# Attention with cluster masks: running sums in SBUF, separate product banks, logits in a score tile, and numbering at the head of a pair

## The chip, the cores and the metric

The kernel runs on one core of a Trainium2 chip. The metric is the device time of one execution in microseconds (us); lower is better. The engines are named as in the profile: PE (TensorE), ACT (ScalarE), DVE (VectorE), POOL (GpSimd) and SP (SyncE, which here issues nearly all DMAs).

## The reference

Routing attention over 4 batches, 8 heads, 768 positions and 64 dimensions is followed by a two-layer network with a squared ReLU. All is float32.

```python
q_assign = argmax(q_n @ c_n.T); k_assign = argmax(k_n @ c_n.T)    # 16 clusters per head
mask = q_assign[:, :, :, None] == k_assign[:, :, None, :]
scores = where(mask, scale * q @ k.T, -1e9)
attn = softmax(scores); x = attn @ v          # then (B*S, H*D) = 3072 x 512
out = square(maximum(x @ w_in, 0)) @ w_out    # w_in 512 x 2048, w_out 2048 x 512
```

## The kernel before

The order of the instructions is written out by hand: each engine runs its instructions in the order of the code and blocks at the first one whose inputs aren't there. That holds for SP too, so a DMA that waits holds all DMAs behind it.

**Attention** goes over 16 pairs of heads (p = 0 to 15; one pair is two heads of one batch, side by side in 128 partitions). The scores stand transposed: keys in the partitions, queries in the columns. A pair has nine score tiles of two banks (ps_sc, three buffers): tiles 0 to 5 hold one block of 128 keys by 512 queries for both heads, tiles 6 to 8 hold two blocks of keys by the last 256 queries. For each tile (tile_of, L558) PE multiplies mask rows (L450) and q, k (L441), and ACT takes the exponential (L457) into one of nine ex tiles. After the nine tiles PE multiplies the exponentials with v (times_v, L474): 24 products of 512 columns into bank V, then 24 of 256 columns into bank M. ACT copies each result into xT (evict, L483). V and M are the two halves of one tile of two banks, vm.

**Sums.** DVE adds the exponentials up over the keys (add, L460): five adds of 128x1024 for tiles 0 to 5 run in vm and the fifth writes total; three more adds take tiles 6 to 8 through part into total. At the end of the pair PE sums total over its partitions (add_up, L492) into M; at the start of the next pair DVE transposes and inverts these (invert, L501, L505), and SP sends them out and back, spread over the partitions (far_r, L507; rb, L510). finish (L520) multiplies them into xT in the next pair.

**Masks.** The cluster of each position comes from logits (L334, PE), a transpose of these (turn_logits, L344, DVE) and number (L346 to L392, DVE), which writes the clusters as small marks. SP writes the marks out (far, L382) and reads them back as six rows (rows, L387), which the masks of the next pair multiply. Pair 0 has its masks turned by PE instead (turn_onehot).

**Turned q and k.** Pairs 0 and 1 are turned by PE (turn_first, turn). From pair 2 on ACT splits q and k into 16-bit words (split_words, L314), SP writes these (L315) and reads them back with a transposing DMA (turn_words, L326).

**Weights.** In each pair one block of 128x512 of w_in is rounded in three steps: round_1 on ACT (L138, L139), round_2 on DVE (L145, L148, L152) and round_3 on POOL (L160). load_ahead (L130, SP) loads the blocks into three buffers, so block p + 2 needs the buffer of block p - 1, which round_3(p - 1) frees.

**The network** comes after attention, as seven products of halves in place of eight (L739 up, L791 down) for four blocks; the first block is multiplied while the rest of the weights is rounded.

In the loop over p, SP's order in one pair from pair 2 on is: second words (L315), q and k (L99), the transposing read for pair p + 2 (L326), v (L109), far_r (L507), two rb (L510), first words (L315), far (L382), six rows (L387), weights (L130), and again the second words. The quotation below has the line numbers of the profile.

Of the kernel before, what the change touches and what calls it, by code (L numbers as in the profile page):

```python
# [18 lines left out]
P = 128  # L19
# [6 lines left out]
def kernel(  # L26
# [44 lines left out]
    expp = att.enter_context(tc.tile_pool(name="expp", bufs=9))  # L71
    accp = att.enter_context(tc.tile_pool(name="accp", bufs=1))
    ps_sc = att.enter_context(tc.tile_pool(name="ps_sc", bufs=3, space=PSUM))
    ps_vm = att.enter_context(tc.tile_pool(name="ps_vm", bufs=1, space=PSUM))
    vm = ps_vm.tile([P, 2, 512], F32, name="vm")
    V, M = vm[:, 0], vm[:, 1]


    BY_PE = 2
# [63 lines left out]
    def round_2(i):  # L143
        dst, lo, hi = of_block(i)
        nc.vector.scalar_tensor_tensor(  # L145
            out=lo, in0=hi, scalar=0x80000000, in1=lo, op0=ALU.bitwise_and, op1=ALU.bitwise_or
        )
        nc.vector.tensor_scalar(  # L148
            out=hi.bitcast(F32), in0=dst.bitcast(F32), scalar1=2.0 ** -15, scalar2=HIGHEST,
            op0=ALU.max, op1=ALU.min,  # L150
        )
        nc.vector.tensor_scalar(  # L152
            out=dst, in0=hi, scalar1=3, scalar2=None, op0=ALU.logical_shift_left
        )

    def round_3(i):
        dst, lo, hi = of_block(i)
        raw_w.pop(i)
        dst, lo = dst.bitcast(I32), lo.bitcast(I32)
        nc.gpsimd.tensor_tensor(out=dst, in0=dst, in1=lo, op=ALU.add)  # L160
# [61 lines left out]
    def fixed_rows():  # L222
        for i, (row, value) in enumerate(((2.0, 1.0), (0.0, -BIG))):
            nc.vector.tensor_scalar(
                out=fixed[:, i : i + 1], in0=row_i[:, 1:2], scalar1=row, scalar2=value,
                op0=ALU.is_equal, op1=ALU.mult,
            )
        for t in rows_of:
            nc.gpsimd.memset(t, 0.0)
            for i in range(2):  # L230
                nc.vector.tensor_scalar(
                    out=t[:, i], in0=t[:, i], scalar1=fixed[:, i : i + 1], scalar2=None,
                    op0=ALU.add,
                )
# [31 lines left out]
    def centroids_turned():  # L266
        nc.tensor.transpose(
            out=M[:, 0:P], in_=cn.rearrange("p e d -> p (e d)"), identity=ident
        )
        nc.vector.tensor_copy(out=cnT, in_=M[:, 0:P])  # L270
# [4 lines left out]
    def turn_first(which):  # L275
        if which == 0:
            qkT[0] = qktp.tile([P, 2 * NCH, P], F32, name="qkT")
        pt = ps_sc.tile([P, 2, 512], F32, name="sc")
        for c in range(NCH):
            nc.tensor.transpose(  # L280
                out=pt[:, c // NB, (c % NB) * P : (c % NB + 1) * P], in_=raw[0][which][:, c],
                identity=ident,
            )
        for i, copy in enumerate((nc.scalar.copy, nc.vector.tensor_copy)):
            c = NCH * which + NB * i
            copy(out=qkT[0][:, c : c + NB].rearrange("p c n -> p (c n)"), in_=pt[:, i, 0:TB])
        if which == 1:
            raw.pop(0)

    def turn(pair, part, bank):  # L290
        if part == 0:
            qkT[pair] = qktp.tile([P, 2 * NCH, P], F32, name="qkT")
        for i in range(4):
            which, c = divmod(4 * part + i, NCH)
            nc.tensor.transpose(
                out=bank[:, P * i : P * (i + 1)], in_=raw[pair][which][:, c], identity=ident
            )
        (nc.scalar.copy if part == 2 else nc.vector.tensor_copy)(
            out=qkT[pair][:, 4 * part : 4 * part + 4].rearrange("p c n -> p (c n)"), in_=bank
        )  # L300
        if part == 2:
            raw.pop(pair)
# [28 lines left out]
    def logits(pair, bank):  # L331
        hp = pair % HP
        for g in range(4):
            nc.tensor.matmul(  # L334
                bank[32 * g : 32 * g + 32, 0:TB], lhsT=cnT[:, 2 * C * hp : 2 * C * (hp + 1)],
                rhs=qkT[pair][:, NB * g : NB * (g + 1)], start=True, stop=True,
            )


    lt = {}  # L340

    def turn_logits(pair, bank):
        lt[pair] = once.tile([P, 2 * NBL, C], F32, name="lt")
        nc.vector.transpose(out=lt[pair].rearrange("p n c -> p (n c)"), in_=bank[:, 0:TB])  # L344

# [48 lines left out]
    def turn_onehot():  # L394
        spare = expp.tile([P, 2, 512], F32, name="ex").bitcast(BF16)
        ohT[0] = spare.rearrange("p a n -> p (a n)")[:, 0 : 2 * S].rearrange(
            "p (a n) -> p a n", a=2
        )
        half = NBL // 2
        for part, bank in ((0, V), (1, M)):  # L400
            po = bank.bitcast(BF16)[:, 0 : half * P].rearrange("p (b g i) -> p b g i", b=half, g=4)
            for b in range(half):
                nc.tensor.transpose(
                    out=po[:, b].rearrange("p g i -> p (g i)"),
                    in_=oh[:, half * part + b].rearrange("p e c -> p (e c)"), identity=ident_b,
                )
            for which in range(2):
                dst = ohT[0][:, which].rearrange("p (g b i) -> p b g i", g=2, b=NBL)
                dst = dst[:, half * part : half * (part + 1)]
                src = po[:, :, 2 * which : 2 * which + 2]  # L410
                if which == 0:
                    nc.vector.tensor_copy(out=dst, in_=src)
                else:
                    nc.scalar.activation(out=dst, in_=src, func=ACT.Copy, bias=-BIG, scale=BIG)
# [16 lines left out]

    def begin(i):
        sc[i] = ps_sc.tile([P, 2, 512], F32, name="sc")


    def score(pair, i, j, first):
# [135 lines left out]

    centroids_norm()
    turn_first(0)
    centroids_turned()
    turn_first(1)
    logits(0, V)
    turn_logits(0, V)
    number(0)
    fixed_rows()  # L580

    first_sums = []
    x_early, w_early = x_sums(FEED[0]), []
    for p in range(NG):
        load_qk(p + 3)
        load_ahead(0)
        if p:
            turn_words(p + 2)
        load_v(p + 1)
        if p == HP + 1:  # L590
            nc.sync.dma_start(x_far, xT.pop(0))
        if p:
            invert(p - 1)
        if 2 < p + 1 < NG:
            turn_logits(p + 1, V)
        if p:
            round_2(p - 1)
            round_3(p - 1)


        if p == 0:
            for i in range(NB):
                begin(i)
                score(p, i, 0, True)
            turn_onehot()
            for i in range(NB):
                mask(p, i, 0, False)
                exponential(i)
            for i, bank in enumerate((V, M, V)):
                turn(1, i, bank)  # L610
        else:
            for i in range(NB):
                tile_of(p, i)
        if p < 2:
            logits(p + 1, M)
            turn_logits(p + 1, M)
        total[p] = endp.tile([P, 2, S], F32, name="total")
        first, last = total[p][:, :, 0:QA], total[p][:, :, QA:S]
        add(nc.vector, vm, ex[0], ex[1])
        add(nc.vector, vm, vm, ex[2])  # L620
        for i in range(NB, NCH):
            tile_of(p, i)
            add(nc.vector, vm if i < NCH - 1 else first, vm, ex[i])
        if p == 0:
            split_words(2, 0)
            split_words(2, 1)
            turn_words(2)
        split_words(p + 3, 0)
        if p + 1 < NG:
            number(p + 1)  # L630


        for i in range(NCH, NCH + NB):
            tile_of(p, i)
        load_ahead(p)
        part = accp.tile([P, 2, 512], F32, name="part")
        add(nc.vector, part, ex[NCH], ex[NCH + 1])
        add(nc.vector, part, part, ex[NCH + 2])
        add(nc.vector, last, part[:, :, 0:QB], part[:, :, QB : 2 * QB])
        if p:  # L640
            finish(p - 1)
        round_1(p)


        for i in range(NCH):
            times_v(p, i, V)
        evict(p, 0, V)
        split_words(p + 3, 1)
        for i in range(NCH, NCH + NB):
            times_v(p, i, M)  # L650
        raw_v.pop(p)
        if 2 < p + 2 < NG:
            logits(p + 2, V)
        evict(p, NCH, M)
        if p + 1 < NG:
            add_up(p, M)
        for d in (qkT, ohT):
            d.pop(p)
        if p >= NG - 2:
            for _ in range(2):  # L660
                if (found := next(x_early)) is not None:
                    first_sums.append(found)
            w_early.append(w_sums(len(w_early)))
# [390 lines left out]
```

## Time and profile before

| what | us |
|---|---|
| median of 3 runs (988.16 to 990.62) | 989.4 |
| the profiled execution | 983.46 |
| its span, first to last instruction | 981.7 |
| attention, from the start to the end of pair 15's v products | 386.5 |
| first up products, with the rounding of weights, to | 475.6 |
| the rest of the products, to the end | 981.7 |

Some rows of the costliest groups (line, engine, operation, output<-input, shape, count, then busy us and mean ns):

| group | busy us | mean ns |
|---|---|---|
| L457 ACT ex<-sc 128x1024, 144 times | 144.4 | 1025 |
| L441 PE sc<-qkT, 768 times, in pairs that run side by side | 160.7 | 501 |
| L474 PE vm<-ex,v_raw, 768 times, likewise | 130.9 | 490 |
| L460 DVE vm<-vm,ex 128x1024, 48 times | 59.2 | 1233 |
| L460 DVE vm<-ex 128x1024, 16 times | 24.1 | 1505 |
| L460 DVE part<-part,ex 128x1024, 16 times | 19.6 | 1225 |
| L460 DVE part<-ex 128x1024, 16 times | 19.0 | 1188 |

How to read it: a time in such a table is that of the engine alone; whether it counts depends on what waits for it. A row of waits names the engine and line that waited, after the arrow who released it, then us in total, how often, and the longest. In a list by time the first column is the start in us from the beginning of the span and the second the length; SPq is the queue in which SP issues DMAs, and its length is that of the issue, not of the transfer. In a list by stretches the columns are the length, busy us and number of instructions of PE, PE's weight loads, DVE, ACT and POOL, the granted clock, the share of the DMA engines and GB/s. From part 6 of the page: one words transfer is 384 KB, one block of weights 512 KB, q, k and v 384 KB each, rb 192 KB each, a row 1.5 or 3 KB.

### The profile page before, as it was taken

How to read it: one execution, taken by the hardware profiler on the slowest of the kernel's cores; microseconds unless marked ns; L12 is line 12 of the kernel's file. 1: busy time of each engine (PE TensorE's matmuls, PEld its weight loads, DVE VectorE, ACT ScalarE, POOL GpSimd, SP SyncE). 2: the span in 40 equal slices, each digit the busy share in tenths (PEclk: the TensorE clock that was granted, in tenths of full speed). 3: DMA queues.
4: the chain of work that ended last, by engine and by line, in shares of the span. 5: the costliest groups of instructions: out<-in, count | busy, mean ns of one | idle time of the engine just before them, and what ended most of it. 6: DMA issues, size and time to landing. Idle time of an engine off the chain costs nothing.

```text
span 981.7 us, 11662 instructions
## 1 busy us (share of the span) xinstructions
PE 920.3 (94%) x4471; PEld 594.8 (61%) x4471; DVE 580.1 (59%) x905; ACT 313.3 (32%) x455; POOL 148.3 (15%) x171
## 2 busy tenths in 40 slices
PE   6789997998998899899899999999999999999997
PEld 4344443554344444456788655888556888556886
DVE  5657775776777776699933565532566531656331
ACT  3555664665756445288000111000111000111000
POOL 2000100000000022475001331002231002231000
PEclk8899998999999999999999999999999999999999
DMA  8356666565566421243100000000000000000000
GB/s 226 82 134 171 197 180 194 153 180 168 153 172 164 105 70 47 81 140 101 60 22 22 22 1 1 11 22 21 11 1 0 22 22 22 1 0 1 22 23 24
DMA packets 102495, 74.80 MB, mean 76 GB/s; under 512 B 60064, under 2 KB 93088, under 8 KB 102176
## 3 DMA queue, kind: packets, MB, share of 16 engines
q1 hardware_dynamic: 100720, 73.55, 26.6%
q8 instruction: 37, 0.61, 0.3%
q10 hardware_dynamic: 1712, 0.43, 0.2%
q14 instruction: 26, 0.21, 0.1%
HBM read 43.73 MB, written 19.22 MB: 64 GB/s over the span
## 4 chain that ended last, share of the span: by engine, by line
PE 65%; DVE 17%; DMA 6%; ACT 5%; SPq 3%; issue 3%; POOL 0%; DVEq 0%; ACTq 0%; POOLq 0%
PE bank L791 29%; PE bank L739 23%; DVE vm L460 7%; PE vm L474 7%; ACT ex L457 3%; PE sc L441 3%; DMA far<-marks_t 3%; SPq L387 3%; DVE g L698 2%; DVE total L460 2%; DMA rows<-far 2%; DVE w_raw L148 1%; DVE w_raw L145 1%; PE sc L450 1%; DMA far_r<-seen 1%
## 5 line engine op out<-in xcount | busy, mean ns | idle before, releaser
L457 ACT ACTIVATE ex<-sc 128x1024 f32<-128x1024 f32 x144 | 144.4, 1025 | 65.1 <-PE sc L441 60.6
L698 DVE TENSOR_TENSOR g<-bank,g 128x384 f32<-128x384 f32 x192 | 103.4, 555 | 98.8 <-PE bank L739 91.2
L441 PE MATMUL sc<-qkT 64*128 64x512 f32 (+1 forms) x768 | 160.7, 501 | 0.0
L474 PE MATMUL vm<-ex,v_raw 128*64 128x512 f32 (+1 forms) x768 | 130.9, 490 | 19.9 <-ACT xT L483 11.6
L791 PE MATMUL bank<-w_out,g 128*128 128x256 f32 x576 | 127.3, 379 | 3.7 <-DVE g L532 3.7
L791 PEld LDWEIGHTS bank<-w_out,g 128*128 128x128 f32 x576 | 109.2, 190 | 19.8 <-DVE g L532 4.1
L474 PEld LDWEIGHTS vm<-ex,v_raw 128*64 128x64 f32 x768 | 52.3, 137 | 97.6 <-issue 45.7
L698 DVE TENSOR_TENSOR osb<-bank,osb 128x256 f32<-128x256 f32 x72 | 29.4, 423 | 134.6 <-PE bank L791 124.0
L441 PEld LDWEIGHTS sc<-qkT 64*128 64x128 f32 x768 | 79.0, 192 | 34.9 <-issue 27.8
L739 PE MATMUL bank<-xT,w_in 128*128 128x384 f32 x256 | 94.0, 490 | 3.2 <-DVE g L698 3.2
L739 PE MATMUL bank<-xT,w_s 128*128 128x384 f32 x256 | 94.1, 491 | 0.0
L739 PE MATMUL bank<-x_t,w_s 128*128 128x384 f32 x256 | 93.0, 486 | 0.0
L791 PE MATMUL bank<-w_t,g_s 128*128 128x256 f32 x384 | 86.8, 379 | 0.0
L791 PE MATMUL bank<-w_t,g 128*128 128x256 f32 x384 | 86.8, 379 | 0.0
L450 PE MATMUL sc<-rows 64*128 64x512 bf16 (+1 forms) x360 | 73.4, 329 | 13.2 <-DMA rows<-far 13.2
L552 POOL TENSOR_TENSOR w_s<-w_in 128x256 f32<-128x256 f32 x32 | 25.2, 789 | 363.2 <-PE bank L791 226.4
L791 PEld LDWEIGHTS bank<-w_t,g 128*128 128x128 f32 x384 | 73.0, 190 | 9.9
L791 PEld LDWEIGHTS bank<-w_t,g_s 128*128 128x128 f32 x384 | 73.0, 190 | 9.9
L702 ACT COPY osb<-bank 128x256 f32<-128x256 f32 x12 | 4.5, 372 | 219.0 <-PE bank L791 219.0
L160 POOL TENSOR_TENSOR w_in<-w_in,w_raw 128x512 int32<-128x512 int32 x16 | 20.9, 1308 | 349.8 <-DVE w_in L152 349.8
L739 PEld LDWEIGHTS bank<-xT,w_in 128*128 128x128 f32 x256 | 48.4, 190 | 37.4 <-DVE g L698 4.1
L702 ACT COPY g<-bank 128x384 f32<-128x384 f32 x32 | 15.2, 475 | 173.8 <-PE bank L739 173.8
(122 smaller groups left out, 997.3 us busy)
## 6 DMA issues: line engine op xcount, KB each, us to landing
words<-flat SPq DMA_DIRECT2D x28, 384.0 KB
w_raw<-in_moe_w_in_dram SPq DMA_DIRECT2D x16, 512.0 KB
w_raw<-in_moe_w_out_dram SPq DMA_DIRECT2D x16, 512.0 KB
v_raw<-in_v_dram SPq DMA_DIRECT2D x16, 384.0 KB
rb<-far_r SPq DMA_DIRECT2D x32, 192.0 KB
out_dram<-osb SPq DMA_DIRECT2D x23, 256.0 KB
q_raw<-in_q_dram SPq DMA_DIRECT2D x14, 384.0 KB
k_raw<-in_k_dram SPq DMA_DIRECT2D x14, 384.0 KB
```

The source lines that it names most:

```text
L160: nc.gpsimd.tensor_tensor(out=dst, in0=dst, in1=lo, op=ALU.add)
L387: nc.sync.dma_start(rows[D * e + row : D * e + row + 1, which].rearrange("p w (g b i) -> p (w g) b i", g=2, b=NBL), mine[2 * which.start : ...
L441: nc.tensor.matmul(sc[i][:, e, cols], lhsT=qkT[pair][rows, NCH + c], rhs=qkT[pair][rows, n.start // P : n.stop // P], start=first, stop=no ...
L450: nc.tensor.matmul(sc[i][:, e, cols], lhsT=ohT[pair][rows, 1, c * P : (c + 1) * P], rhs=ohT[pair][rows, 0, columns(i)], start=first, stop= ...
L457: nc.scalar.activation(out=ex[i], in_=sc.pop(i), func=ACT.Exp, scale=SCALE)
L460: eng.tensor_tensor(out=out, in0=a, in1=b, op=ALU.add)
L474: nc.tensor.matmul(bank[D * e : D * (e + 1), 0 : n.stop - n.start], lhsT=raw_v[pair][:, e, c], rhs=ex[i][:, e, cols], start=c == 0, stop=c ...
L552: nc.gpsimd.tensor_tensor(out=s1, in0=a[1][0], in1=a[1][1], op=ALU.add)
L698: nc.vector.tensor_tensor(out=out, in0=bank, in1=to, op=ALU.add)
L702: nc.scalar.copy(out=c11, in_=bank)
L739: nc.tensor.matmul(bank, lhsT=operands[j][0][:, kk], rhs=operands[j][1][:, kk], start=(kk == 0), stop=(kk == H2 - 1),)
L791: nc.tensor.matmul(bank, lhsT=left[:, f], rhs=right[:, f], start=(f == 0), stop=(f == F2 - 1))
```

## The change

- V and M become two tiles of one bank each (av_a, av_b) instead of halves of one tile.
- The running sum of tiles 0 to 5 stands in total, in SBUF, from the first add on.
- A tenth score tile is taken in each pair but the last: its bank 0 holds the logits of pair p + 2, its bank 1 the sums of pair p. add_up stands ahead of evict of M.
- number(p + 1) stands at the head of pair p, behind turn_logits, instead of behind the fifth add; for pairs 1 and 2 it stands behind the first add of the pair before. Its seven DMAs move with it in SP's order, ahead of both words.
- round_2 and round_3 of block p - 1 move from the head of pair p to behind finish. The load of block p + 2 now stands ahead of them in the code; on SP it waits for this pair's round_3.
- At the start both halves of pair 0 are turned first, all copies of turned pairs but one go to ACT, pair 1 is turned between the first scores of pair 0, fixed_rows stands behind the exponentials, and of the words of pairs 2 and 3 only the first stand ahead of the last three tiles.

```diff
-    ps_vm = att.enter_context(tc.tile_pool(name="ps_vm", bufs=1, space=PSUM))
-    vm = ps_vm.tile([P, 2, 512], F32, name="vm")
-    V, M = vm[:, 0], vm[:, 1]
+    ps_av = att.enter_context(tc.tile_pool(name="ps_av", bufs=1, space=PSUM))
+    V, M = (ps_av.tile([P, 512], F32, name=f"av_{i}") for i in "ab")
...
-        for i, copy in enumerate((nc.scalar.copy, nc.vector.tensor_copy)):
+        for i in range(2):
+            copy = nc.vector.tensor_copy if which and i else nc.scalar.copy
...
-        (nc.scalar.copy if part == 2 else nc.vector.tensor_copy)(
+        nc.scalar.copy(
...
-    def turn_logits(pair, bank):
+    def turn_logits(pair):
+        bank = sc["ls"][:, 0]
...
     centroids_norm()
     turn_first(0)
+    turn_first(1)
     centroids_turned()
-    turn_first(1)
-    logits(0, V)
-    turn_logits(0, V)
+    logits(0, begin("ls"))
+    turn_logits(0)
     number(0)
-    fixed_rows()
...
         if 2 < p + 1 < NG:
-            turn_logits(p + 1, V)
-        if p:
-            round_2(p - 1)
-            round_3(p - 1)
+            turn_logits(p + 1)
+            number(p + 1)
...
             for i in range(NB):
+                if i < 2:
+                    turn(1, i, (V, M)[i])
+                else:
+                    turn_onehot()
                 begin(i)
                 score(p, i, 0, True)
-            turn_onehot()
+                if i == 1:
+                    turn(1, 2, V)
             for i in range(NB):
                 mask(p, i, 0, False)
                 exponential(i)
-            for i, bank in enumerate((V, M, V)):
-                turn(1, i, bank)
+            fixed_rows()
...
-        if p < 2:
-            logits(p + 1, M)
-            turn_logits(p + 1, M)
...
-        add(nc.vector, vm, ex[0], ex[1])
-        add(nc.vector, vm, vm, ex[2])
+        add(nc.vector, first, ex[0], ex[1])
+        if p < 2:
+            logits(p + 1, begin("ls"))
+            turn_logits(p + 1)
+            number(p + 1)
+        add(nc.vector, first, first, ex[2])
         for i in range(NB, NCH):
             tile_of(p, i)
-            add(nc.vector, vm if i < NCH - 1 else first, vm, ex[i])
-        if p == 0:
-            split_words(2, 0)
-            split_words(2, 1)
-            turn_words(2)
-        split_words(p + 3, 0)
-        if p + 1 < NG:
-            number(p + 1)
+            add(nc.vector, first, first, ex[i])
+        split_words(2 if p == 0 else p + 3, 0)
...
         if p:
             finish(p - 1)
+            round_2(p - 1)
+            round_3(p - 1)
+        if p == 0:
+            split_words(2, 1)
+            turn_words(2)
+            split_words(3, 0)
         round_1(p)
...
-        if 2 < p + 2 < NG:
-            logits(p + 2, V)
+        if p + 1 < NG:
+            bank = begin("ls")
+            if 2 < p + 2:
+                if p + 2 < NG:
+                    logits(p + 2, bank)
+            add_up(p, bank[:, 1])
         evict(p, NCH, M)
-        if p + 1 < NG:
-            add_up(p, M)
```

More of the change, by code (lines that the diff above doesn't have):

```diff
@@ L334, in logits @@
             nc.tensor.matmul(
-                bank[32 * g : 32 * g + 32, 0:TB], lhsT=cnT[:, 2 * C * hp : 2 * C * (hp + 1)],
+                bank[32 * g : 32 * g + 32, 0, 0:TB], lhsT=cnT[:, 2 * C * hp : 2 * C * (hp + 1)],
                 rhs=qkT[pair][:, NB * g : NB * (g + 1)], start=True, stop=True,
@@ L433, in begin @@
         sc[i] = ps_sc.tile([P, 2, 512], F32, name="sc")
+        return sc[i]
     def score(pair, i, j, first):
```

## The prediction

> **What bounds the kernel now.** I read the page first, then TensorE's waits, then SyncE's own queue in order of time, then the stretches by clock.
>
> From the page, part 1, the busy times by engine, and from part 2 the granted clock:
>
> ```profile
> PE 920.3 (94%) x4471; PEld 594.8 (61%) x4471; DVE 580.1 (59%) x905; ACT 313.3 (32%) x455; POOL 148.3 (15%) x171
> ...
> PEclk8899998999999999999999999999999999999999
> ```
>
> TensorE is close to full over the span, but the average hides two parts. From 475.6 to the end (506.1 us) it is busy for 500.5 us in dense products that the change doesn't touch. All that can be won lies in attention, 0 to 386.5 us. There the waits of TensorE (total us, times, longest) are:
>
> ```profile
> PE sc L450 <- DMA rows<-far: 13.2, 11, 2.5
> PE vm L474 <- ACT xT L483: 11.6, 16, 1.3
> PE vm L474 <- DVE total L460: 8.4, 15, 1.0
> PE vm L492 <- ACT xT L483: 7.3, 15, 0.5
> ```
>
> The last three, 27.3 us, come from the shared tile vm: a pair waits 0.96 us for the last sum (first v product), 0.69 for the copy of V and 0.49 for that of M. From 96.21 to 117.98 one pair takes 21.77, so TensorE's own work in it is 21.77 - 2.14 = 19.63. That looks like a gain of 2.1 us a pair. The first row speaks against it: in 11 pairs TensorE waited for the mask rows, which come through SyncE. SyncE's queue over one pair (start, us, line):
>
> ```profile
> 95.30 0.46 SPq L315 DMA_DIRECT2D words<-flat  x1
> ...
> 100.30 3.21 SPq L326 DMA_TRANSPOSE qkT<-words  x1
> 103.61 0.53 SPq L109 DMA_DIRECT2D v_raw<-in_v_dram  x1
> 104.23 0.41 SPq L507 DMA_DIRECT2D far_r<-seen  x1
> 107.10 1.14 SPq L510 DMA_DIRECT2D rb<-far_r  x2
> 108.30 0.58 SPq L315 DMA_DIRECT2D words<-flat  x1
> 110.02 0.34 SPq L382 DMA_DIRECT2D far<-marks_t  x1
> 112.28 3.98 SPq L387 DMA_DIRECT2D rows<-far  x6
> 116.37 0.35 SPq L130 DMA_DIRECT2D w_raw<-in_moe_w_in_dram  x1
> 116.77 0.43 SPq L315 DMA_DIRECT2D words<-flat  x1
> ```
>
> This is a closed loop, because SyncE issues in order and blocks: words to transposition 5.0 (the words must land; 4.8 to 5.4 in all pairs from pair 2 on), its issue 3.3, v 0.6, far_r to rb 2.9, two rb 1.2, words 0.6, far to rows, six rows 4.1, weights 0.4. Far to rows is 1.5 to 2.3 where far follows words late and 3.4 where it follows at once (202.89 to 206.32). With 3.4 the loop is 21.5, beside 21.77 for TensorE with its waits. So two loops of one length run side by side, and pulling 2.1 us out of one leaves the other.
>
> **The change part by part.**
> Waits on vm: the products get two tiles, the sums go to another bank, the running sum leaves PSUM. All three waits go. What is late next is the rows, so in pairs 2 to 13 this is worth nothing by itself.
>
> Sums in SBUF: five adds a pair. The nearest rows have both inputs in SBUF already: part<-ex 1188 ns, part<-part,ex 1225, against vm<-vm,ex 1233. I take no difference. One rule speaks against it. The Trainium skill (SBUF — State Buffer, "Who interferes with whom") says that a VectorE instruction with two SBUF inputs is shut out by a GpSimd one that reads SBUF. The trace has it: the first add is the only one of the five with two such inputs, and it took 1.96 beside round_3's add, 1.23 in pairs without it.
>
> ```profile
> 99.28 1.28 POOL L160 TENSOR_TENSOR w_in<-w_in,w_raw 128x512 int32<-128x512 int32 x1 [20.48 <-DVE w_in L152]
> 99.70 1.96 DVE L460 TENSOR_TENSOR vm<-ex 128x1024 f32<-128x1024 f32 x1 [0.50 <-ACT ex L457]
> ```
>
> By the rule all five adds are exposed, up to 1.3 each; by the rows GpSimd has one such add a pair, and the change puts it behind the round after the last add, where VectorE next reads PSUM. So between +1.3 and -0.7 a pair on VectorE; I take -0.7. VectorE's list in a pair: transposes and reciprocal 1.5, numbering 3.1 (106.92 to 110.00), five adds at 1.34, three part adds 3.2, to 14.6 us after the pair's start; then it must wait for rb.
>
> Logits and sums in a score tile: the third score tile of a pair now waits for the transposes, done 1.49 after the start (97.70 against 96.21), while that tile begins at 2.16 (98.37). Behind it would stand all of TensorE, but 0.7 is left. Cost nothing; if VectorE came late, one for one.
>
> Numbering first: its VectorE work (3.1) fits into what the start of a pair loses, round_2 (1.6), and the wait for the second exponential. Its seven DMAs move ahead of the first words on SyncE. So SyncE no longer waits for VectorE before far (waits of 1.0 to 2.4 in five pairs), and words now follow the rows, 1.0 us ahead of the second words, with the 512 KB of weights between. Far then goes right behind rb; pair 13, which has no words, shows that: 338.84 to 341.79, 2.95. The words in a row: 384 KB more lie ahead of those that the transposition waits for. Before, the data began 0.75 after the second words' issue and ended near 4.05; now it begins 0.6 earlier and carries 384 KB more at the 300 GB/s of the stretches 97 to 99: +1.2 - 0.6 = +0.6. Ends: 0.2 (the queue starts early enough) and 1.8 (384 KB alone, 48.99 to 52.22 less the fixed part). I take 0.6.
> New loop: 21.5 - 0.45 + 0.6 = 21.65. For the eleven pairs from 72.40 to 324.35, each pair's own loop less its wait for VectorE, far at 2.95 or, where it was 3.4, half a us less, plus 0.6: 0.0, +0.25, +0.2, +0.1, -1.9, +0.1, +0.2, +0.1, +0.1, +0.1, +0.05, together -0.7.
>
> round_2 and round_3 moved: the weight load on SyncE now waits for this pair's GpSimd add, with the second words, the next q and k and the transposition queued behind it. From the first rb: landing 4.0 (224.08 to 228.07, also on an idle queue, 398.87 to 402.87), finish 1.5, round 1.6, GpSimd 1.4: at 8.6; SyncE gets there at 1.2 + 2.95 + 4.1 + 0.6 = 8.85. A margin of 0.25: free, but only just.
>
> The start: turning pair 1 moves under numbering 0; the masks of pair 0 begin at 18.2 as before, since they wait for the one-hot turns. Then exponentials to 21.0, add 1.3, transpose 0.7, numbering 3.1: far at 26.0 (before 42.26, as SyncE sat behind words and transposition of pair 2). Rows 27.5 to 31.6; two words; landed at 36.5 (768 KB at some 270 GB/s, as 256 and 289 in the stretches 36 to 38, with 1.1 us ahead of the data and 0.95 behind); transposition issued to 39.4, its data to 42.1 (5.6 from its start, as 38.63 to 44.2); words of pair 3, landed 45.8; issue 4.7 as before, 50.5; far_r 51.1, rb 54.05, far 55.3, rows 58.25 to 62.3, second words at 63.4 against 72.40: -9.0. TensorE is not in the way: pair 1 starts near 37, waits for transposed pair 2 until 43, ends near 60.5.
>
> The end: pair 13 still has the words ahead of its transposition, +0.6. Pairs 14 and 15 have none, TensorE sets them: 0.23 + 0.68 + 0.47 + 0.50 + 0.68 = 2.6 of waits go. Against that stands the clock. The Trainium skill (TensorE: Matmul & The Clock Gate, "What's actually happening") halves it after about 3.4 us of idling. The trace halves it after less: waits of 2.38 and 1.32 around 165, and 1.63 at 234.7.
>
> ```profile
> 163.00:164.00 1.00, 0.04 (x1) 0.07 (x1) 0.97 (x3) 0.00 (x0) 0.00 (x0) 0.56 0.02 2
> ...
> 236.00:237.00 1.00, 1.00 (x6) 0.50 (x4) 0.00 (x0) 0.00 (x0) 1.00 (x1) 0.50 0.97 329
> ```
>
> From the start of the pair to its first v product that cost 12.12 and 11.78 instead of 10.84, 1.1 on average. By the rule, waits of some 2.2 a pair cost nothing; by the rows, 1.1 a pair. Where the rows set the pace, it only shortens the next wait; in pair 14 it counts: -2.6 + 1.1 = -1.5. After that the products' work is unchanged and shifts whole.
>
> Sum: -9.0 - 0.7 + 0.6 - 1.5 = -10.6. The profiled execution, 983.46 with a span of 981.7, becomes 972.9. It lies 5.9 under the median of 989.4, so the median forecast is 978.8.
>
> **The rivals.** (1) TensorE's waits go and the rows come in time: 19.63 a pair, about 2 us on twelve pairs more, 954. For it: three waits plainly removed. Against it: the loop of SyncE needs neither engine. 5%.
> (2) The words in a row cost 0.2 and transfers are quicker: 0.4 to 0.6 a pair on twelve pairs, 972. 18%.
> (3) The start gives little, because the turns of pair 1 crowd the one-hot banks or half clock stretches pair 0: far(1) some 6 to 8 us later, 986 to 988. 13%.
> (4) Slower: SyncE is held by the weight load. VectorE reaches finish at 14.6 and rb lands near 16.2; if adds, shared ports or the late start make VectorE more than 1.85 late (1.6 + the margin), each further us is a us on twelve pairs. From 0.9 a pair the gain is gone; adds at 1.96 instead of 1.23 (3.65 a pair) give 1.8 a pair, 978.8 + 21.6 = 1000. With the words at 1.8 as well this side begins earlier (1.2 x 12 = 14.4, 993). 18%.
> (5) My sum, 974 to 984: 46%.
>
> **How the numbers follow.** A measurement of this kernel can tell about 0.3%, 3 us, from no change. Faster by more (under 986.4): (1), (2), (5) and part of (3), 0.70. Within: the rest of (3) and the edge of (4), 0.13. Slower: 0.17. The range 968 to 992 takes in both ends of the words and the start, and leaves out (1) and the far part of (4).
>
> **What would show it.** Right: no waits of v products on the sums; TensorE's waits for rows up from 13.2 to about 25; pair to pair still 21.5 to 23; far(1) near 26 and the second words of pair 2 near 63; words to transposition near 5.6. Wrong: pairs at 20 or under (SyncE is no bound), or the weight load starting well after the last row with GpSimd as its releaser, or far(1) after 32.

## The result and the profile after

The changed kernel takes 975.0 us in the median (973.4 to 976.6, 4 runs) beside 989.7 for the kernel before (988.2 to 990.6, 4 runs): a ratio of 0.9853, interval 0.9831 to 0.9875, or 14.7 us less. Run twice more on other chips it gave 0.9869 (0.9839 to 0.9898) and 0.9855 (0.9828 to 0.9881). Its profiled execution took 975.83 with a span of 974.0; the one of before had taken 983.46.

From the page of the changed kernel, busy times by engine and granted clock in 40 slices:

```profile
PE 923.0 (95%) x4471; PEld 613.3 (63%) x4471; DVE 579.6 (60%) x902; ACT 315.1 (32%) x458; POOL 148.8 (15%) x171
...
PEclk8999989999989999999999999999999999999999
```

No engine has less to do than before. What has changed is the waits of TensorE (total, times, longest):

```profile
PE sc L452 <- DMA rows<-far: 30.5, 20, 2.4
PE bank L797 <- DVE g L534: 3.7, 1, 3.7
PE bank L745 <- DVE g L704: 3.3, 1, 3.3
PE sc L334 <- DMA qkT<-words: 2.1, 1, 2.1
```

The three waits on vm, 27.3 us before, are gone, and the wait for the mask rows has grown from 13.2 to 30.5. The second and third rows lie behind attention and stood there before. TensorE waits 10 us less in all, but the middle pairs of heads are no shorter (the table below). The reason is in SyncE's queue. Here is its loop from the second words of one pair to those of the next (start, length of issue):

```profile
110.40 0.68 SPq L315 DMA_DIRECT2D words<-flat  x1
...
115.81 2.87 SPq L326 DMA_TRANSPOSE qkT<-words  x1
118.77 0.53 SPq L108 DMA_DIRECT2D v_raw<-in_v_dram  x1
119.40 0.40 SPq L509 DMA_DIRECT2D far_r<-seen  x1
122.52 1.14 SPq L512 DMA_DIRECT2D rb<-far_r  x2
123.71 0.58 SPq L383 DMA_DIRECT2D far<-marks_t  x1
127.99 3.95 SPq L388 DMA_DIRECT2D rows<-far  x6
132.04 0.39 SPq L315 DMA_DIRECT2D words<-flat  x1
132.47 0.54 SPq L129 DMA_DIRECT2D w_raw<-in_moe_w_in_dram  x1
133.11 0.68 SPq L315 DMA_DIRECT2D words<-flat  x1
```

Far follows rb at once, as forecast, words to transposition take 5.41, and the turn is 22.7 long. SyncE is still the bound of the middle pairs. The gain lies at both ends of attention. The same queue at the start:

```profile
27.62 0.33 SPq L383 DMA_DIRECT2D far<-marks_t  x1
29.09 4.09 SPq L388 DMA_DIRECT2D rows<-far  x6
...
38.19 2.88 SPq L326 DMA_TRANSPOSE qkT<-words  x1
...
63.56 0.67 SPq L315 DMA_DIRECT2D words<-flat  x1
```

The marks of pair 1 go out at 27.62 instead of 42.26, and the second words of pair 2 at 63.56 instead of 72.40. Attention taken apart at three marks, for all profiles of the two kernels (us; the last column is the rest of the span; "second words of pair 2" are those that SyncE issues in pair 2):

| profile | second words of pair 2 | from there to those of pair 13 | to the first up product | rest |
|---|---|---|---|---|
| before | 72.40 | 251.95 | 62.08 | 595.3 |
| before, second | 72.42 | 254.61 | 62.83 | 598.3 |
| after | 63.56 | 255.38 | 58.04 | 597.0 |
| after, second | 62.25 | 256.27 | 57.72 | 598.3 |
| after, third | 62.58 | 257.63 | 58.10 | 597.0 |

Start: 9 to 10 us won. Eleven middle pairs: about 3 lost. End: 4 to 5 won. The rest, which the change doesn't touch, differs by up to 3 us by itself.

### The profile page after: what moved, and what is told of

Same layout as the page of the kernel before. It is cut to its first block, busy times and chain, and to the rows that moved or that the text cites. A ratio compares the mean times of both kernels' runs of the same rounds, so it can differ in the third digit from the quotient of the medians.

```text
span 974.0 us, 11635 instructions
## 1 busy us (share of the span) xinstructions
PE 923.0 (95%) x4471; PEld 613.3 (63%) x4471; DVE 579.6 (60%) x902; ACT 315.1 (32%) x458; POOL 148.8 (15%) x171
## 4 chain that ended last, share of the span: by engine, by line
PE 66%; DMA 12%; DVE 9%; SPq 6%; ACT 3%; issue 3%; POOL 0%; DVEq 0%; ACTq 0%; POOLq 0%
PE bank L797 29%; PE bank L745 23%; PE sc L443 9%; SPq L388 5%; DMA far<-marks_t 4%; DMA far_r<-seen 4%; DMA rows<-far 3%; PE sc L452 2%; DVE total L462 2%; DVE g L704 2%; ACT ex L459 1%; DVE w_raw L147 1%; DVE w_raw L144 1%; PE av_a L476 1%; SPq L512 1%
## 5 line engine op out<-in xcount | busy, mean ns | idle before, releaser
L443 PE MATMUL sc<-qkT 64*128 64x512 f32 (+1 forms) x768 | 172.2, 522 | 0.0
L452 PE MATMUL sc<-rows 64*128 64x512 bf16 (+1 forms) x360 | 83.9, 344 | 30.6 <-DMA rows<-far 30.5
L443 PEld LDWEIGHTS sc<-qkT 64*128 64x128 f32 x768 | 89.6, 201 | 29.0 <-issue 25.5
L476 PE MATMUL av_a<-ex,v_raw 128*64 128x512 f32 x384 | 85.9, 597 | 0.0
L462 DVE TENSOR_TENSOR total<-total,ex 128x1024 f32<-128x1024 f32 x64 | 78.3, 1224 | 7.3 <-ACT ex L459 1.1
L452 PEld LDWEIGHTS <-rows 64*128 64x128 bf16 x360 | 33.0, 98 | 63.6 <-issue 42.7
```

What stands on the lines that cost most here:

```text
L443: nc.tensor.matmul(sc[i][:, e, cols], lhsT=qkT[pair][rows, NCH + c], rhs=qkT[pair][rows, n.start // P : n.stop // P], start=first, stop=no ...
L452: nc.tensor.matmul(sc[i][:, e, cols], lhsT=ohT[pair][rows, 1, c * P : (c + 1) * P], rhs=ohT[pair][rows, 0, columns(i)], start=first, stop= ...
L462: eng.tensor_tensor(out=out, in0=a, in1=b, op=ALU.add)
L476: nc.tensor.matmul(bank[D * e : D * (e + 1), 0 : n.stop - n.start], lhsT=raw_v[pair][:, e, c], rhs=ex[i][:, e, cols], start=c == 0, stop=c ...
```

## The experiments

My theory: SyncE's closed loop sets the pace of pairs 2 to 13, so neither the freed banks nor the order shortens a pair, and what is won is won at the start. The rivals: the waits on vm were the bound, or the order of the numbering is what pays. All runs are compared with the kernel before on the same chip.

**Before, unchanged.**

> The kernel before, unchanged. Its profiled execution (983.46 us) lies 5.9 us under the median of its timed runs; that of the changed kernel (975.83) lies on its median. My theory: an execution of the kernel before varies in how far the waits for mask rows stretch and how often the clock halves behind them, and the profiled one was a good one; a second profile then lies at 986 to 990 and shows more waits for rows than 13.2 us or a lower granted clock than 0.983. Rival: the profile itself shifts the time; then the second profile is again near 983 beside timed runs near 989.

991.2 us, ratio 0.9993 (0.9971 to 1.0014); its profiled execution took 989.95, with 15.4 us of waits for rows: the theory's range. So the first profile of before, 983.46, on which the forecast's sum was made, was a low one: 3.4 us quicker in attention, and 3.0 in the rest, which the theory did not have. What two profiles differ by is known to some 3 us here, not better.

**The waits alone:** two banks, sums in SBUF, logits and sums in a score tile; start and order as before.

```diff
+    V, M = (ps_av.tile([P, 512], F32, name=f"av_{i}") for i in "ab")
...
+        add(nc.vector, first, ex[0], ex[1])
```

> The kernel before with only the banks changed: v products in two tiles, running sum in SBUF, logits and sums in a score tile. Numbering, rounds and the start stay where they were. My theory: TensorE no longer waits 27.3 us for sums and copies, and nearly all of it comes back as waits for the mask rows, since SyncE's loop (about 21.5 us a pair) is untouched; 3 to 5 us faster at most, 985 to 989, waits for rows from 13 to 30 us or more. Rival (the waits on vm set the pace): 2 us a pair over 15 pairs, 955 to 962.

983.9 us, ratio 0.9940 (0.9908 to 0.9972): a little under the theory's 985 to 989, far from the rival. TensorE's waits for rows:

```profile
PE sc L450 <- DMA rows<-far: 39.0, 22, 6.7
```

The 27.3 us of waits on vm have come back as 26 us more of waits for rows, and the eleven middle pairs take 254.2, inside the two values of before. The gain of about 6 us is mostly at the start: second words of pair 2 at 67.70, 4.7 earlier. That the banks help there was not in my forecast. In the kernel before, the turns of pair 0's masks and of pair 1 wait for the shared tile at the start (its waits of TensorE):

```profile
PE vm L403 <- ACT ex L414: 1.9, 1, 1.9
PE vm L295 <- DVE qkT L298: 1.6, 2, 0.9
```

From 14 to 30 us TensorE's waits are 5.6 in the kernel before and 2.4 here, and the first v product starts at 29.95 instead of 34.97.

**The order alone:** numbering at the head, round_2 and round_3 behind finish; shared tile, sums in PSUM and start as before.

```diff
         if 2 < p + 1 < NG:
             turn_logits(p + 1, V)
-        if p:
-            round_2(p - 1)
-            round_3(p - 1)
+            number(p + 1)
...
         if p:
             finish(p - 1)
+            round_2(p - 1)
+            round_3(p - 1)
```

> The kernel before with only the order inside a pair changed: numbering at the head, round_2 and round_3 behind finish; one tile for both banks, sums in PSUM and the start as before. Theory: the order by itself is worth nothing in the pairs (numbering ahead of the first add makes the last sum late, the v products wait longer for it, words come 0.6 later), 986 to 996. Rival (the order is what makes rows come in time): 974 to 982.

994.0 us, ratio 1.0026 (1.0002 to 1.0049): as the theory had it, and by a hair on the slow side. TensorE's waits:

```profile
PE vm L474 <- DVE total L460: 13.3, 15, 3.7
PE sc L450 <- DMA rows<-far: 12.2, 10, 2.6
PE vm L474 <- ACT xT L483: 11.6, 16, 1.3
```

The wait for the last sum grew from 8.4 to 13.3, as numbering now stands ahead of the first add; 2.9 of the 4.9 is one wait in pair 1. There SyncE also waits 5.0 for GpSimd's rounding, and the second words of pair 2 go out at 75.55, 3.1 later than before. By itself the order is worth nothing; what it does together with the banks comes below.

**The start alone**, in the kernel before:

```diff
     turn_first(0)
+    turn_first(1)
     centroids_turned()
...
+        if p == 0:
+            logits(1, M)
+            turn_logits(1, M)
+            number(1)
         add(nc.vector, vm, ex[0], ex[1])
```

> The kernel before with the start of the changed one (turns, copies, numbering 1 and words of pair 0 as there; one tile for both banks, order of later pairs as before). Theory (an earlier start shifts the loop, which keeps its length): the marks of pair 1 go out near 26 to 29, second words of pair 2 at 64 to 67 instead of 72.4, and the shift stays: 5 to 8 us faster, 982 to 986. Rival (later waits swallow the shift, since the products with the shared tile keep 21.77 a pair): within 3 us of before, 988 to 994.

985.0 us, ratio 0.9928 (0.9910 to 0.9945): the time is as the theory had it, but its step is not. The marks of pair 1 did go out early, at 29.68, yet the second words of pair 2 only at 69.67, 2.7 earlier instead of 5 to 8. Two things stand in the way. One is the products in the shared tile (TensorE's waits from 20 to 64):

```profile
PE vm L475 <- DVE total L461: 5.0, 2, 4.2
PE vm L404 <- ACT ex L415: 1.0, 1, 1.0
PE vm L475 <- ACT xT L484: 0.7, 1, 0.7
```

The 4.2 is the first v product of pair 0, which starts at 36.60 here and at 29.37 in the changed kernel. (Here the numbering of pair 1 stands ahead of the first add, in the changed kernel behind it.) The other is the order: the numbering of pair 2 still stands behind the fifth add, so SyncE waits 4.0 for its marks after rb, as it did before. In the changed kernel far follows rb at once (54.25 and 55.46).

```profile
57.63 1.16 SPq L511 DMA_DIRECT2D rb<-far_r  x2
63.77 0.34 SPq L383 DMA_DIRECT2D far<-marks_t  x1
```

Each alone, the banks win 4.7 up to the second words of pair 2, the start wins 2.7 and the order loses 3.1, together 4.3. The changed kernel wins 8.8, so about half of it comes only when the three stand together.

**The start put back**, all else as changed, run on two chips:

> The changed kernel with the start of the kernel before: pair 1 is turned behind the first masks, numbering of pair 1 behind the fifth add, the words of pairs 2 and 3 ahead of it. From pair 1 on as changed. My theory: the second words of pair 2 are issued 8 to 9 us later than in the changed kernel (63.6), and the time is 8 to 10 us above it, 983 to 985. Rival (the gain is made in the pairs, not at the start): 975 to 978.

980.4 us, ratio 0.9879 (0.9835 to 0.9922); second words of pair 2 at 69.67, 6.1 later than in the changed kernel and not 8 to 9. The time lies between the theory (983 to 985) and its rival (975 to 978): neither was right.

> The changed kernel with the start of before, once more, with more rounds and the changed kernel beside it. Theory: the start is worth 4 to 8 us in the time, as the second words of pair 2 lie 6 us apart. Rival: 0 to 3 us, the distance is lost in later pairs.

> The changed kernel beside the two others, as their reference: 973 to 979 by all theories.

981.9 us, ratio 0.9902 (0.9873 to 0.9932), beside 977.1 and 0.9855 (0.9828 to 0.9881) for the changed kernel on the same chip: 4.7 us by the medians, as the theory had it, though the intervals overlap a little. The second words of pair 2 lie at 68.83 and 62.58. Not all of these 6 us is kept: with the start put back the eleven middle pairs take 253.2 and 253.3, in the changed kernel 255.4 to 257.6. Most of that stands in pair 2, where words to transposition takes 7.1 to 7.4 in the changed kernel, and 5.0 and 4.6 with the start put back. Why the words land late there is open.

Without the start the change is worth about 1.0 to 1.2%, of which banks and sums alone give 0.6 (the intervals overlap). The profiles place what the order adds at the end: from the second words of pair 13 to the first up product it is 59.6 and 58.2 with the start put back, but 63.1 with the waits alone. There the marks of pair 15 still go out behind the fifth add of pair 14, and TensorE waits 2.1 for their rows; in the changed kernel they go out 11 us earlier and it doesn't wait (first the waits alone, then the changed kernel):

```profile
358.76 0.33 SPq L381 DMA_DIRECT2D far<-marks_t  x1
...
347.39 0.53 SPq L383 DMA_DIRECT2D far<-marks_t  x1
```

**The rows off SyncE:** marks and rows (seven DMAs a pair) issued by GpSimd, to test the loop itself.

```diff
-        nc.sync.dma_start(far.rearrange("g r f i -> (g r) f i"), turned)
+        nc.gpsimd.dma_start(far.rearrange("g r f i -> (g r) f i"), turned)
...
-                nc.sync.dma_start(
+                nc.gpsimd.dma_start(
```

> The changed kernel with the marks' way out and the six rows issued from GpSimd's queue instead of SyncE's. My theory: SyncE's loop loses some 8 us of issue and waiting and is no bound any more; TensorE sets the pace at 19.6 to 20 us a pair, waits for rows fall from 30.5 us to under 5, and the time falls by 2.5 us a pair on 12 pairs, to 940 to 950. Rival (the pace is set by VectorE or by the transfers themselves, not by the queue): pairs stay at 22 us or over and the time stays within 5 us of 975; a third way is that issue from GpSimd is so slow that rows come late anyway, and then waits for rows stay and GpSimd shows them.

968.2 us, ratio 0.9770 (0.9730 to 0.9809): faster, but far from 940 to 950. TensorE's waits for rows are gone, and a second loop stands in their place (waits of TensorE, of SyncE's queue and of VectorE):

```profile
PE sc L452 <- DVE lt L345: 28.5, 12, 6.0
...
PE sc L452 <- DMA rows<-far: 1.3, 2, 0.7
...
SPq L129 <- POOL w_in L159: 121.6, 16, 12.7
...
DVE xT L522 <- DMA rb<-far_r: 61.8, 14, 8.9
```

This is the chain of my fourth rival: finish waits for rb, round_3 on GpSimd for finish, the weight load on SyncE for round_3, and behind it stand the second words, the transposition, and the next rb. (Of the 121.6, 81.9 lie between 50 and 325 us, where the changed kernel has none; in all it has 26.6.) The chain was just covered by the first loop and becomes the bound when that goes. Its end on TensorE is the price that I had set for the logits in a score tile "if VectorE came late, one for one": the mask rows' tile waits for the transposed logits, because VectorE sits in finish.

**The weights behind the second words**, rows on SyncE as in the changed kernel, with the changed kernel beside it:

```diff
     for p in range(NG):
+        if p:
+            load_ahead(p - 1)
         load_qk(p + 3)
...
-        load_ahead(p)
+        if p == NG - 1:
+            load_ahead(p)
```

> The changed kernel, nothing altered, beside the three below. Both theories: 972 to 978 us. Its second profile shows how much of the difference of two profiles is chance: waits of TensorE for rows 25 to 36 us (30.5 in the first), second words of pair 2 at 63.5 +- 0.5, eleven pairs to 319 +- 3.

> The changed kernel with the load of the weights behind the second words in place of ahead of them. Theory (the pace of a pair is SyncE's closed loop): 512 KB less lie ahead of the words that the transposition waits for, so words to transposition falls from 5.5 to about 4.0, and the loop by 1.5 on eleven pairs: second words of pair 13 some 14 to 17 us earlier, time about 958, waits of TensorE for rows near 10. Rival (the transfers are shared anyway, or the transposition itself then shares the queues with the weights): the loop is within 0.4 of before a pair, 970 to 978.

976.8 us, ratio 0.9837 (0.9806 to 0.9868), beside 978.2 and 0.9869 (0.9839 to 0.9898) for the changed kernel: not told apart, so the rival was right. (The changed kernel's second words of pair 2, at 62.25, missed the 63.5 that was expected of them by more than the 0.5 allowed; its waits for rows, 32.4, did not.) One turn of SyncE's queue:

```profile
108.26 0.98 SPq L315 DMA_DIRECT2D words<-flat  x2
109.33 0.83 SPq L129 DMA_DIRECT2D w_raw<-in_moe_w_in_dram  x1
...
112.84 5.43 SPq L326 DMA_TRANSPOSE qkT<-words  x1
118.37 0.53 SPq L108 DMA_DIRECT2D v_raw<-in_v_dram  x1
```

The words do land earlier: words to transposition is 4.18 in the median instead of 5.54, as forecast. But now the issue of the transposition holds SyncE for 5.55 instead of 3.26, and over eleven pairs the one falls from 63.5 to 46.6 in sum and the other rises from 36.4 to 61.5.

**Both together**, rows on GpSimd and weights behind the words:

> As the run with marks and rows issued by GpSimd, and the load of the weights behind the second words as well. Theory: with GpSimd's rounding no longer ahead of the words on SyncE, both holders of the loop are gone, TensorE sets the pace at 19.6 to 20.5 a pair, 938 to 952. Rival (a loop remains: rb waits for the transposition on SyncE, finish on VectorE waits for rb, the numbering behind it): 955 to 968.

949.8 us, ratio 0.9574 (0.9548 to 0.9600): the theory's range. With both holders gone every pair but one (27.8) takes 18.5 to 21.4, where the theory had 19.6 to 20.5, so its rival's loop is still there in part. What is left of TensorE's waits:

```profile
PE sc L452 <- DVE lt L345: 14.5, 8, 5.8
PE sc L452 <- DMA rows<-far: 6.2, 7, 1.6
```

**The sums off SyncE as well** (far_r and rb issued by GpSimd):

> As the run with marks and rows on GpSimd's queue and late weights, and the sums (far_r, rb) issued by GpSimd too. Theory (what is left there of waits, 14.3 us for VectorE's transposed logits, comes from rb standing behind the transposition on SyncE): waits of TensorE for lt under 4, pace 19.6 to 20.4 a pair, 936 to 945. Rival (GpSimd's own queue becomes the holder: rows behind rb, rounding behind rows): rows late again, 948 to 960.

942.2 us, ratio 0.9510 (0.9488 to 0.9531): the theory's range again, and the quickest version, 4.9% under the kernel before and about 35 us under the changed one. TensorE no longer waits for lt at all. All that it waits for between 60 and 341, and two stretches from the v products of one pair to those of the next, one in the middle and the last (length, then busy times and instructions of PE, PEld, DVE, ACT, POOL, granted clock, DMA share, GB/s):

```profile
PE sc L452 <- DMA rows<-far: 9.7, 7, 2.2
PE sc L452 <- issue: 1.2, 1, 1.2
```

```profile
106.09:125.22 19.13, 19.13 (x138) 8.95 (x137) 16.07 (x24) 13.90 (x18) 7.02 (x11) 1.00 0.77 187
314.87:333.35 18.48, 18.48 (x130) 8.75 (x128) 16.61 (x18) 11.33 (x14) 11.55 (x14) 1.00 0.19 48
```

Seven of the fifteen pairs take 19.12 or 19.13, full of TensorE's work at full clock. That is the floor which the forecast's first rival had set at 19.63; to reach it, two chains of DMAs and a weight load got out of SyncE's way; the waits on vm alone did not do it. What the same moves would give in the kernel before, with its shared tile, was not run.

## Why the prediction was right, and where it was not

The time was right, and the mechanism too: SyncE's loop takes up what the freed waits give. But two terms were mis-sized with opposite signs, the anchor was low, and that the number came out so near is in part luck.

**Waits on vm worth nothing in the middle pairs: right.** The run with the waits alone keeps the pace, and its waits for rows take up what vm gave back.

**Sums in SBUF free: right.** The groups of VectorE's adds in the changed kernel (busy us, mean ns | idle):

```profile
L462 DVE TENSOR_TENSOR total<-total,ex 128x1024 f32<-128x1024 f32 x64 | 78.3, 1224 | 7.3 <-ACT ex L459 1.1
...
L462 DVE TENSOR_TENSOR total<-ex 128x1024 f32<-128x1024 f32 x16 | 19.5, 1220 | 30.8 <-ACT ex L459 30.7
```

1224 against 1233 for the same add in PSUM, and the first add 1220 in the mean where 1505 stood. The second comes from the order and not from SBUF: in the run with the order alone, sums in PSUM, the first add takes 1215. The rule of the Trainium skill (SBUF — State Buffer, "Who interferes with whom") is not refuted: the change put round_3 behind the last add, so only one of these adds still stands beside it, by 0.1 us. With the waits alone, where round_3 stays at the head, five of the later adds stand beside it, and four of these took 1.57.

**The start, -9.0: right in size (-8.8, and -9.8 to -10.2 in the other profiles), with a condition that it doesn't name.** In the changed kernel the steps come as forecast: marks at 27.62 (26.0), the issue of the second transposition done at 50.16 (50.5), second words at 63.56 (63.4). But "TensorE is not in the way" holds only with the banks, and the early far of pair 2 only with the order; the start alone brings 2.7.

**The middle pairs, -0.7: wrong in sign, +3.4.** This is the step that failed. The loop of eleven pairs, taken apart (us, sums):

| piece of the loop | before | before, second | after | after, second | forecast of the change |
|---|---|---|---|---|---|
| second words to transposition | 55.5 | 53.5 | 63.5 | 62.1 | +6.6 |
| issue of the transposition | 36.2 | 39.1 | 36.4 | 39.6 | 0 |
| far_r to rb | 39.8 | 41.8 | 42.0 | 39.8 | 0 |
| rb to far | 30.0 | 29.0 | 13.1 | 13.3 | words and waits for VectorE go |
| far to rows | 31.9 | 32.7 | 35.1 | 36.2 | at 2.95, 32.5 |
| end of rows to second words | 5.9 | 5.9 | 13.0 | 13.0 | the first words come here |

The words cost 0.54 a pair in the median (5.0 to 5.54; forecast 0.6), but the sum is +8.0, as pair 2 alone has +2.4 (4.99 to 7.40); with the start put back pair 2 hasn't got it, and the eleven pairs take as long as before. So the early start gives a part of its gain back, which the forecast did not have. Rb to far shrank to 1.19 as forecast. The other mis-sized piece is far to rows, taken as 2.95 from one pair without words: it is 3.19 a pair in the mean, 2.6 over the eleven pairs. Far_r to rb adds 2.2 in this profile and nothing in the second, so that part is chance. Against the second profile of before the whole loss is 0.8 to 3.0.

**round_2 and round_3, a margin of 0.25: right.** GpSimd's add in the turn before the one shown, and the weight load that waits for it:

```profile
108.32 1.28 POOL L159 TENSOR_TENSOR w_in<-w_in,w_raw 128x512 int32<-128x512 int32 x1 [21.98 <-DVE w_in L151]
```

```profile
109.76 0.54 SPq L129 DMA_DIRECT2D w_raw<-in_moe_w_in_dram  x1
```

The add ends at 109.60, the load goes out at 109.76: 0.16, and 0.05 to 0.16 in all middle pairs but one. SyncE did not wait for GpSimd there in this profile; in the third it did twice, 1.5 us in all. (The four terms of the forecast make 8.5 and not 8.6.) The rival that made this the slow case was real, as the run with the rows on GpSimd shows, but it comes to next to nothing while the other loop is the longer.

**The end, -0.9 in all (+0.6 - 1.5): too small, -4.0.** From the v products of pair 13 to those of pair 14 it is now 19.83 instead of 21.80, and to pair 15's 18.48 instead of 20.50: two pairs, not one, got the whole 2.0 of the freed waits. (In the second profile the first of these is 21.41, though the end as a whole is as short, 57.72.) With the waits alone the end is no shorter than before, so this gain needs the order as well, which the forecast did not say. The charge of 1.1 for the clock was not due: with nothing to wait for, the clock stayed at 1.00 in both.

**The anchor.** The sum in the profile was to be -10.6; the profiles give -8.84 + 3.4 - 4.0 = -9.4 in attention, and the rest took 1.7 more. I then added 5.9, the distance of the low profile of before from its median. The changed kernel's profiles (975.83, 976.26, 977.1) have no such distance, so 978.8 came out only 3.8 high, because two errors met: the forecast for the profile, 972.9, was 2.9 too low, and the distance added to it too high by more. The gain by the ratios is 13 to 15 us, by the mean of the profiles 10.3; the difference is the scatter of two profiles of before, and I can't assign it to a step.

**A reading that was wrong.** The row of 13.2 us of waits for mask rows has 11 waits in eight pairs; it does not say that TensorE waited for rows in 11 pairs. From the v products of pair 2 to those of pair 5, at 21.77 a pair, it waited for none. The two loops were as close as forecast, but in these pairs TensorE's own was the longer.

## What to carry to other kernels

When two loops of one length run side by side, removing the waits from one moves them to the other: find the second loop in the queue's own timeline before counting the waits as gain. When one engine issues nearly all DMAs in order and each waits for the one before, it can pay to give a chain of small, dependent DMAs to another engine's queue, and to look for the next loop behind it: here the ratio to the kernel before went from 0.985 to 0.977 with the first chain, to 0.957 with the second holder gone, and to 0.951 with the second chain. An early start pays only as far as the stages behind it can take it; here it needed the banks and the order. And a part that is worth nothing alone can be worth something beside another, as the order was at the end of attention.

## What was not expected of the hardware

**The issue of a transposing DMA has no fixed length.** It held SyncE 3.26 us in the median with 512 KB of weights ahead of the words, 5.55 with them behind the words, and 6.0 in the two quickest versions. That it waits for transfers under way fits these three, but other causes were not tried. (The profile puts 32.5 us of the changed kernel's eleven waits at this line down to TensorE, L443; whether that is a real wait was not tried either.) In the start the issue took 2.88 for the first transposition, and 4.22 for the second, which follows q and k.

**Waits gathered in one place came with a lower clock.** With the waits on vm gone, TensorE runs ahead and then waits in one place. The pair from 73.61 to 99.57 (columns as above):

```profile
82.00:83.00 1.00, 1.00 (x16) 0.13 (x4) 1.00 (x2) 0.00 (x0) 0.00 (x0) 1.00 0.00 0
83.00:84.00 1.00, 0.00 (x0) 0.00 (x0) 1.00 (x2) 0.00 (x0) 0.00 (x0) 1.00 0.03 3
84.00:85.00 1.00, 0.00 (x0) 0.00 (x0) 0.93 (x4) 0.00 (x0) 0.00 (x0) 1.00 0.02 2
85.00:86.00 1.00, 0.39 (x1) 0.09 (x1) 0.96 (x3) 0.00 (x0) 0.94 (x1) 1.00 0.04 4
...
88.00:89.00 1.00, 0.91 (x3) 0.66 (x5) 0.96 (x3) 0.00 (x0) 0.00 (x0) 0.60 0.90 240
89.00:90.00 1.00, 1.00 (x5) 0.42 (x3) 0.25 (x2) 0.00 (x0) 0.00 (x0) 0.50 1.13 281
```

Two waits of over 2 us with one matmul between them, and the next 3 us ran at half clock. From 60 us to the end of attention the mean granted clock fell from 0.98 (both profiles of before) to 0.93 to 0.95 (the three of the changed kernel and the run with the waits alone), and is 0.98 to 0.99 in the two quickest versions, where most of these waits are gone. Pairs take anything from some 20 to 26 us, where before most came every 21.77. How much of this the wait for rows hides was not measured.
